# Chunks three to five of a decay attention in blocks of 64 tokens, and a first product in two column groups

## The chip, the cores and the metric

The kernel runs on one core of a Trainium2 chip. Its engines work side by side, each through its own list of instructions in order: PE (TensorE, matrix products into PSUM), ACT (ScalarE), DVE (VectorE), POOL (GpSimd) and SP (SyncE, which issues the DMAs). An instruction waits only for what it names by semaphores, and everything behind it on its engine waits with it. The metric is the device time of one execution in microseconds (us), as the median of the runs shown. Execution before: 538.77 us (three runs, 538.08 to 539.0).

## The reference

Three stages, of which the change touches the first and the start of the second:

```python
for b in range(nb):                       # blocks of 64 tokens, 8 heads, D = 64
    intra = (qb @ kb.T * Dmask) @ vb      # Dmask[i, j] = lam ** (i - j) for i >= j
    inter = (qb * lam_pow) @ kv_state
    out[b] = intra + inter
    kv_state = lam_block * kv_state + (kb * rev_pow).T @ vb
h = x @ w_in;  x = (h * tanh(softplus(h))) @ w_out     # 512 -> 2048 -> 512
h = x @ w2_in; x = (h * sigmoid(h)) @ w2_out           # 512 -> 2048 -> 512
```

There are 2 batches of 768 tokens, 1536 tokens in all. The recurrence over blocks is linear, so the block length is free: with 128 tokens per block (and the matching powers of lam) the result is the same.

## The kernel before

**Attention.** The 1536 tokens are 12 chunks of 128, counted here from 0 as in the code (0 to 5 are the first batch). Eight heads stand as four pairs. For every chunk PE makes four kinds of product: the scores `s` = k x q; the state product `pc` = decayed keys `kd` x v; and the chunk's output `px`, from two products, one of the masked scores `sm` with v and one of the state with the decayed queries `qd`. DVE masks the scores (`sm`) and adds up the states; POOL makes `qd`, half of `kd` (heads 4 to 7) and the decay of the state; ACT makes the other half of `kd` (heads 0 to 3, four instructions, L352). Then ACT rounds the output to its high part `xh` (L541) and DVE takes the low part `xl` = output - `xh` (L546). These are the operands of the feed-forward, tiles of 512 tokens, four chunks each.

There are two ways through a chunk. **Whole** (`whole_S`, `whole_px`, `whole_out`, `whole_state`): one block of 128 tokens; `s` and `px` are products over 128 columns (L364, L407, L417), the decay of keys and masks are read from `whole_mask`, and a chunk's state is one addition. **In blocks of 64** (`emit_S`, `emit_pc`, `emit_intra`, `emit_inter`, `emit_mid`, `emit_state`): two blocks of 64, so each product is made of pieces of 64 x 64 on 64 rows (L458, L474, L508, L522); a state in the middle of the chunk (`mid`, DVE) is needed for the second block, a short `touch` (DVE) follows `px`, `fade` (POOL) is the decayed old state, and `kd` is made with `dmask`, a rearranged copy of the mask that ACT writes (L757). The output then lies crosswise in PSUM, and `xh` and `xl` take three pieces instead of one. Before, chunks 0 to 5 are whole and 6 to 11 in blocks of 64 (`PH = 4`, `W = CPS = 6`).

**Feed-forward.** Products are made as three passes of reduced-precision matmuls: high x high, high x low, low x high. `emit_h` (L596) is the first product of one slice of 128 hidden columns for 512 tokens, 12 matmuls of 512 columns; it will be called step i (i = 0, 1, ... ; four slices for each of three tiles of tokens). `emit_u` (L619) is the second product, two steps behind (`LAG = 2`), into the two PSUM banks `ps_o` that the scores use too. After a step ACT applies the activation twice (L577) and DVE takes its low part (L578).

**Weights.** They arrive as 64-bit words and are decoded: "in-weights f" and "out-weights f" for slice f. Each takes two ACT steps (L143, L144, called a pair below), two DVE steps (L176, L180), an ACT cast to the high part (L248) and a POOL subtraction to the low part (L249). `split_w` queues these pieces: `run_pre` takes the next ACT pair, `run_split` the next DVE step, `run_parts` the next cast and subtraction, `pump` the next DMA, each if its input was begun long enough ago (`tick` counts visits).

**Order.** Nothing is reordered by a scheduler: each engine's list is the order in which the Python below calls these functions. In the stretch of the change, SP's list of DMAs is the keys and values of chunks 0 to 3 (each in two halves), in-weights 0 and 1, chunk 4, in-weights 2, chunk 5, out-weights 0, chunk 6, out-weights 1, in-weights 3, chunk 7, out-weights 2 and 3 and so on, each when its buffer is free. From chunk 8 on the attention of a chunk is called inside a first product, before its last two matmuls (`attend`).

Of the kernel before, what the change touches and what calls it, by code (L numbers as in the profile page):

```python
# [7 lines left out]
F32 = mybir.dt.float32  # L8
# [9 lines left out]
def decay_attention_mish_silu_kernel(  # L18
# [26 lines left out]
    PH = 4  # L45
    CPS = N // 2
    W = CPS
# [439 lines left out]
    def emit_state(n):  # L487
        if n >= N:
            return
        pc, mid = pcs.pop(n), mids[n % 2]  # L490
        if n % CPS == CPS - 1:
            return
        for p in range(NP):
            nc.vector.scalar_tensor_tensor(
                out=states[(n + 1) % 2][:, p], in0=mid[:, p], scalar=lamrow[:, p, L - 1 : L], in1=pc[:, 1, p],
                op0=ALU.mult, op1=ALU.add,
            )
        emit_fade(n + 1)
# [81 lines left out]
    def emit_h(t, n, first=False, inside=None):  # L580
# [9 lines left out]
        order = [(*e, kk) for kk in range(KD) for e in early] + [(*lst, kk) for kk in range(KD)]  # L590
# [142 lines left out]
    for n in range(PH):  # L733
        if n > 1:
            whole_state(n)
            whole_px(n)
        if n:
            if n < PH - 1:
                whole_S(n + 1)
            if n == PH - 2:  # L740
                run_pre(1, 0)
                run_split(2, 0)
            whole_out(n)
            if n == PH - 1:
                whole_S(n + 1)
                whole_kd(n + 1)
            whole_qd(n + 1)
            whole_decay(n + 1)
        if n == 1:
            for key in ((0, 0), (1, 0), (2, 0), (0, 1), (1, 1), (3, 0), (2, 1), (3, 1), (4, 0), (5, 0)):  # L750
                split_w(*key, key[0] > 3)
        pump()
        if n == PH - 1:
            run_pre(1, 0)
            run_split(2, 0)
            for c in range(2):
                nc.scalar.copy(dmask[rows[c]], whole_mask[rows[c], :, :, half[c]])  # L757
            run_pre(2, 0)
        run_parts()
        if n < PH - 2:  # L760
            whole_kd(n + 2)
        tick[0] += 1

    for i, (t, f) in enumerate(steps):
        n = i + PH
# [26 lines left out]
        if n >= N:  # L792
            run_sums(SUMS[n - N][0])
        if not W <= n < N:
            run_later()
        lows = len(later)
        if i < LAG:
            run_split(2)
        if n == N - 1:
            emit_pc(n)  # L800
            emit_intra(n)

        def attend():
            if n < N - 1:
                emit_pc(n)
            emit_mid(n)
            if n < N - 1:
                emit_intra(n)
            emit_S(n + 1)
            run_later(lows)  # L810
            emit_inter(n)

        act = emit_h(t, f, f == 0, attend if 8 <= n < N else None)
        if n >= N:
            run_sums(SUMS[n - N][1])
        if i:
            run_parts()
        leave = None
        if n < W:
            if n < W - 1:  # L820
                whole_state(n)
            whole_px(n)
            if n < W - 1:
                whole_S(n + 1)
            whole_out(n)
            if n < W - 1:
                whole_qd(n + 1)
                run_parts()
                if n < W - 2:
                    whole_decay(n + 1)  # L830
                    whole_kd(n + 1)
            else:
                wctx.close()
                homes.append(ctx.enter_context(tc.tile_pool(name="accr", bufs=1, side="right")))
                homes.append(actx.enter_context(tc.tile_pool(name="sp", bufs=2)))
                mids, fades = [
                    [homes[1].tile([P, NP, D], F32, tag=f"{name}{i}", name=f"{name}{i}", bufs=1) for i in range(2)]
                    for name in ("mid", "fade")
                ]
                emit_S(n + 1)  # L840
                emit_kd(n + 1)
                emit_qd(n + 1)
        elif n < N:
            if n < 8:
                attend()
            if n % CPB == CPB - 1:
                out_lows = emit_out(n)
                emit_kd(n + 1)
                emit_qd(n + 1)
                emit_state(n)  # L850
                out_lows()
            run_split(2)
            if i == LAG:
                run_parts()
            if n in pxs:
                emit_kd(n + 1)
                emit_qd(n + 1)
            while due:
                due.pop(0)()
            if n in pxs:  # L860
                emit_state(n)
                emit_out(n)()
        if act:
            act()
        if i >= LAG:
            leave = emit_u(*divmod(i - LAG, 4))
            if n < N:
                run_parts()
            leave()
        if i == LAG - 1:  # L870
            run_pre(1)
            run_split(2)
            run_parts(1)
        run_pre(1 + (i == LAG or n >= N))
# [627 lines left out]
```

## Time and profile before

| what | value |
|---|---|
| median of three runs | 538.77 us |
| the profiled execution's own time | 538.69 us |
| its span (first to last instruction) | 536.9 us |
| busy in the span: PE, PE weight loads, DVE, ACT, POOL | 531.3, 441.7, 438.7, 353.8, 320.6 us |
| granted TensorE clock, mean | 1.000 |
| chain that ended last, by engine | PE 86%, DVE 5%, DMA 4%, ACT 3% |

The times of the rows below count from the start of the span; 1.79 us of the execution lie outside it. A row's second number is the time from the start of its first instruction to the end of its last; instructions on one engine overlap a little at their ends, so how long a group holds its engine is read as the distance to the start of the next group. A matmul's end is modelled, so PE looks busy wherever nothing is said of a wait. Matmuls of float32 without the reduced-precision mark stand as two records each: 16 of the `x16` rows are eight products.

### The profile page before, as it was taken

To read this page: it belongs to the slowest core of one execution; us is meant where nothing else is said; L and a number is where in the kernel's file an instruction comes from. 1 tells how busy PE (TensorE), PEld (TensorE's weight loads), DVE (VectorE), ACT (ScalarE), POOL (GpSimd) and SP (SyncE) were. 2 spreads that over 40 slices of the span, in tenths; PEclk is the share of its full clock that TensorE was granted. 3 is DMA by queue.
4 is the path that set the end of the run, shared out by engine and by line. 5 is a ranking of instruction groups with operands and counts; after the bars stand their busy time and mean duration, and the time that the engine had idled before them with its cause. 6 is when DMAs were issued, how large, how long until landed. Compare 5 with 4: busy or idle time off the path is not lost.

```text
span 536.9 us, 9332 instructions
## 1 busy us (share of the span) xinstructions
PE 531.3 (99%) x3441; PEld 441.7 (82%) x3441; DVE 438.7 (82%) x711; ACT 353.8 (66%) x675; POOL 320.6 (60%) x306
## 2 busy tenths in 40 slices
PE   9999999999999999999999999999999999999997
PEld 6888878878788888888888888888878888888886
DVE  5887968898989895968688989897888786969685
ACT  4788645658574757658587878567684757576562
POOL 3665741349676494757641655958575585775860
PEclk9999999999999999999999999999999999999999
DMA  8994350003212222131301212222212122221106
GB/s 297 402 322 160 121 196 0 2 3 117 79 43 74 80 78 81 58 99 39 105 14 41 79 39 78 80 78 81 73 51 68 45 78 79 79 79 40 40 1 236
DMA packets 14605, 49.88 MB, mean 93 GB/s; under 512 B 1632, under 2 KB 1888, under 8 KB 14560
## 3 DMA queue, kind: packets, MB, share of 16 engines
q1 hardware_dynamic: 14560, 49.29, 26.8%
q8 instruction: 27, 0.44, 0.3%
q14 instruction: 18, 0.15, 0.1%
HBM read 46.14 MB, written 3.15 MB: 92 GB/s over the span
## 4 chain that ended last, share of the span: by engine, by line
PE 86%; DVE 5%; DMA 4%; ACT 3%; issue 1%; SPq 1%; DVEq 0%; ACTq 0%
PE z L1234 20%; PE z L938 15%; PE z L1185 10%; PE zx L938 8%; PE ph L596 5%; PE pu L619 5%; PE zx L1234 4%; PE zx L1003 4%; PE z L1003 4%; PE z L1130 4%; PE zx L1185 3%; DMA xslot<-x 2%; DMA slab<-w 2%; PE zx L1130 2%; DVE acc L1258 1%
## 5 line engine op out<-in xcount | busy, mean ns | idle before, releaser
L249 POOL TENSOR_TENSOR arena<-dec,arena 128x512 fp32r<-128x512 f32 (+1 forms) x51 | 62.8, 1235 | 66.0 <-ACT arena L248 63.9
L1258 DVE TENSOR_TENSOR acc<-z,acc 128x512 f32<-128x512 f32 x135 | 87.1, 685 | 4.5 <-PE z L1234 4.4
L1234 PE MATMUL z<-arena 128*128 128x512 f32 x308 | 85.6, 390 | 0.0
L249 POOL TENSOR_TENSOR arena<-t,arena 128x512 fp32r<-128x512 f32 x46 | 59.9, 1309 | 38.5 <-ACT arena L248 31.6
L1234 PEld LDWEIGHTS z<-arena 128*128 128x128 f32 x308 | 57.7, 188 | 12.2 <-ACT acc L1256 0.3
L248 ACT CAST arena<-dec 128x512 fp32r<-128x512 f32 (+1 forms) x56 | 33.0, 590 | 35.4 <-DVE dec L180 35.0
L248 ACT CAST arena<-t 128x512 fp32r<-128x512 f32 x49 | 30.0, 619 | 35.8 <-POOL t L213 35.8
L938 PE MATMUL z<-xh,arena 128*128 128x512 f32 x182 | 49.6, 392 | 0.0
L1097 POOL TENSOR_TENSOR arena<-F,arena 128x1024 fp32r<-128x1024 f32 x11 | 26.6, 2415 | 34.7 <-PE z L1185 15.1
L213 POOL TENSOR_TENSOR t<-dec 128x256 f32<-128x256 f32 x54 | 42.8, 793 | 6.2 <-DVE dec L180 6.2
L1185 PE MATMUL z<-arena 128*128 128x512 f32 x145 | 42.2, 390 | 0.1
L144 ACT ACTIVATE slot<-slot 128x512 uint32<-128x512 uint32 x58 | 38.6, 665 | 0.0
L938 PEld LDWEIGHTS z<-xh,arena 128*128 128x128 f32 x182 | 32.7, 189 | 5.6
L1234 PE MATMUL z<-more,arena 128*128 128x512 f32 x108 | 35.5, 390 | 0.0
L176 DVE SCALAR_TENSOR_TENSOR z<-z,slot 128x512 uint32<-128x512 uint32 x33 | 22.9, 695 | 12.0 <-ACT slot L144 11.9
L619 PE MATMUL pu<-arena 128*128 128x512 f32 x132 | 32.6, 392 | 0.0
L1185 PEld LDWEIGHTS z<-arena 128*128 128x128 f32 x145 | 27.1, 188 | 6.1 <-DVE arena L1142 0.5
L213 POOL TENSOR_TENSOR t<-dec,t 128x256 f32<-128x256 f32 x40 | 31.5, 788 | 1.0
L596 PE MATMUL ph<-xh,arena 128*128 128x512 f32 x96 | 31.2, 399 | 0.1
L619 PEld LDWEIGHTS pu<-arena 128*128 128x128 f32 x132 | 24.6, 188 | 5.4
L938 PE MATMUL z<-xl,arena 128*128 128x512 f32 x94 | 29.0, 390 | 0.0
L1097 POOL TENSOR_TENSOR arena<-F,more 128x1024 fp32r<-128x1024 f32 x11 | 26.5, 2413 | 0.2 <-PE z L1185 0.2
(312 smaller groups left out, 1433.2 us busy)
## 6 DMA issues: line engine op xcount, KB each, us to landing
slot<-w SPq DMA_DIRECT2D x58, 512.0 KB, 3.7
xslot<-x SPq DMA_DIRECT2D x24, 512.0 KB, 7.0
slab<-w SPq DMA_DIRECT2D x6, 512.0 KB, 6.5
out<-F SPq DMA_DIRECT2D x4, 256.0 KB, 2.9
out<-slot SPq DMA_DIRECT2D x4, 256.0 KB, 2.9
out<-acc SPq DMA_DIRECT2D x3, 256.0 KB, 3.0
out<-acc SPq DMA_DIRECT2D x2, 128.0 KB, 2.4
factors<-lam SPq DMA_DIRECT2D x1, 0.0 KB
```

The lines of the kernel that those rows point to most:

```text
L144: nc.scalar.activation(low, low, AF.Copy, scale=TOP3, bias=2.0**-21 - 0.5)
L213: adder[0].tensor_tensor(out=t[:, k], in0=in0, in1=in1, op=op)
L248: nc.scalar.copy(hi, f)
L249: nc.gpsimd.tensor_tensor(out=lo, in0=f, in1=hi.bitcast(F32), op=ALU.subtract)
L596: nc.tensor.matmul(ph, lhsT=wi[wsel][:, kk * P : (kk + 1) * P], rhs=xt[xsel][:, kk, :], start=(i == 0), stop=(i == 3 * KD - 1),)
L619: nc.tensor.matmul(banks[j], lhsT=wtiles[f, 1][ws][:, js[j] * P : js[j] * P + P], rhs=gts[f, t][gs], start=(i in (0, 2)), stop=(i >= len(p ...
L938: nc.tensor.matmul(self.Z[dst], lhsT=w[ws][:, kk * P : (kk + 1) * P], rhs=x[xx][:, kk, :], start=(start and i == 0), stop=True, skip_group ...
L1003: nc.tensor.matmul(self.Y[dst], lhsT=w[ws][:, kk * P : (kk + 1) * P], rhs=x[xx][:, kk, :], start=(start and i == 0), stop=True, skip_group ...
L1097: low.tensor_tensor(out=lo, in0=f, in1=hi.bitcast(F32), op=sub)
L1185: nc.tensor.matmul(banks[k], lhsT=lhsT, rhs=rhs, start=(j == 0 and ws + gs == 0 and not self.seeded), stop=True, skip_group_check=True,)
L1234: nc.tensor.matmul(self.quad[dst][k], lhsT=w[ws][:, k * P : (k + 1) * P], rhs=g[gs], start=(start and i == 0), stop=True, skip_group_check ...
L1258: tt(out=to, in0=self.quad[src][k], in1=to, op=add)
```

## The change

`PH` becomes 3 and `W` goes: chunks 0 to 2 stay whole, chunks 3, 4 and 5 go in blocks of 64 like 6 to 11. Chunk 3 gets a visit of its own with no first product in it. The order of all pieces from the first chunks to chunk 11 is now written as one string of names per visit. `emit_fade` is no longer called by `emit_state` but is a name in those strings. The first product of step 0 is made over the columns of chunks 0 to 2 (384) first, then over those of chunk 3 (128), for the two passes with high weights, and then over all 512 for the pass with low weights.

```diff
-    PH = 4
+    PH = 3
     CPS = N // 2
-    W = CPS
...
         if n == t == 0:
-            order = [(*e, kk) for e in (early[0], lst, early[1]) for kk in range(KD)]
-        for wsel, xsel, kk in order:
+            order = [(*e, kk, c) for c in (slice(0, T - C), slice(T - C, T)) for e in (early[0], lst) for kk in range(KD)]
+            order += [(*early[1], kk, every) for kk in range(KD)]
+        for wsel, xsel, kk, c in order:
...
             nc.tensor.matmul(
-                ph, lhsT=wi[wsel][:, kk * P : (kk + 1) * P], rhs=xt[xsel][:, kk, :],
-                start=(i == 0), stop=(i == 3 * KD - 1),
+                ph[:, c], lhsT=wi[wsel][:, kk * P : (kk + 1) * P], rhs=xt[xsel][:, kk, c],
+                start=(i == 0), stop=(i == len(order) - 1), skip_group_check=(n == t == 0),
             )
...
+    visits = [
+        "splits wqd decay wS parts dm wout pump wkd",
+        "wstate wpx wout pump pre0",
+        "kd_ S sp0 fade qd sp0",
+        "pc intra mid S inter parts out st outl pump pre0 pre0 sp0 sp0 qd kd fade pre0 parts",
+        "h sp pc qd mid intra sp S sp st inter lows out due kd pre fade outl pump",
+        "parts h pc lows mid intra S inter due out st kd fade sp pre qd outl sp pump part",
+        "h lows pc mid S intra parts pre sp inter sp pump sp st parts pre due kd out outl fade parts qd u leave pump2",
+        "h pc kd lows mid intra S inter st out outl sp qd sp fade due pre u sp leave pre pump1 sp parts parts pre",
...
+    heads, visits = visits[: PH - 1], visits[PH - 1 :]
+    for n in range(1, PH):
+        head(n)
...
+    for i in range(PH - 5, N - 4):
+        visit(i)
```

In a visit of chunk n, `S`, `kd` (also `kd_`), `qd` and `fade` are for chunk n + 1, the rest for n; `wkd` in the visit of chunk n is for n + 2; `h` is the first product of step n - 4, `u` the second two steps behind, `pre`, `sp`, `parts` and `pump` the next pieces of the weights; a 0 behind a name drops the demand for age. `wkd` of the first string makes a whole `kd` for chunk 3 and `kd_` of the third makes it again in blocks of 64.

Three places in the engines' lists carry the prediction. The first is ACT's, from chunk 3's keys on; slot_79 holds in-weights 0, xslot_101 chunk 4, xslot_104 chunk 3. Before:

```order
L352 ACTIVATE kd<-xslot_104,whole_mask 128x64 x4
L143 ACTIVATE dec<-slot_79 128x512
L144 ACTIVATE slot_79<-slot_79 128x512
L541 CAST xh<-px 128x2x128
L541 CAST xh<-px 64x2x128 x2
L248 CAST arena<-dec 128x512
L541 CAST xh<-px 128x4x128
L352 ACTIVATE kd<-xslot_101,whole_mask 128x64 x4
```

And now:

```order
L351 ACTIVATE kd<-xslot_104,whole_mask 128x64 x4
L539 CAST xh<-px 128x2x128
L539 CAST xh<-px 64x2x128 x2
L142 ACTIVATE dec<-slot_79 128x512
L143 ACTIVATE slot_79<-slot_79 128x512
L351 ACTIVATE kd<-xslot_104,dmask 128x64 x4
L247 CAST arena<-dec 128x512
L539 CAST xh<-px 128x4x64
L539 CAST xh<-px 64x4x64 x2
```

Chunk 2's casts have moved ahead of the pair of in-weights 0, chunk 3's `kd` is made a second time behind that pair, and chunk 3's output takes three casts instead of one.

The second place is PE's list around step 0. Before:

```order
L596 MATMUL ph<-xh,arena 128x512 x4
L596 MATMUL ph<-xl,arena 128x512 x4
L596 MATMUL ph<-xh,arena 128x512 x4
L382 MATMUL pc<-xslot_101,kd 64x64 x8
L407 MATMUL px<-qd,state_99 64x128 x8
```

And now:

```order
L596 MATMUL ph<-xh,arena 128x384 x4
L596 MATMUL ph<-xl,arena 128x384 x4
L596 MATMUL ph<-xh,arena 128x128 x4
L596 MATMUL ph<-xl,arena 128x128 x4
L596 MATMUL ph<-xh,arena 128x512 x4
L473 MATMUL pc<-xslot_101,kd 64x64 x16
L506 MATMUL px<-sm,xslot_101 64x64 x16
```

Step 0 has 20 matmuls instead of 12 over the same columns; chunk 4 behind it is 64 pieces instead of 32 products.

The third place is ACT's list where chunk 6's output is cast (the rows with 4x64), xslot_104 being chunk 7. Before:

```order
L248 CAST arena<-dec 128x512
L352 ACTIVATE kd<-xslot_104,dmask 128x64 x4
L541 CAST xh<-px 128x4x64
L541 CAST xh<-px 64x4x64 x2
L627 COPY acc<-pu 128x512 x2
L143 ACTIVATE dec<-slab 128x512
L144 ACTIVATE slab<-slab 128x512
```

And now:

```order
L247 CAST arena<-dec 128x512 x2
L142 ACTIVATE dec<-slab 128x512
L143 ACTIVATE slab<-slab 128x512
L351 ACTIVATE kd<-xslot_104,dmask 128x64 x4
L539 CAST xh<-px 128x4x64
L539 CAST xh<-px 64x4x64 x2
L627 COPY acc<-pu 128x512 x2
```

The pair of out-weights 3 (slab) has moved ahead of chunk 7's `kd` and chunk 6's casts, where it stood behind them. SP's list of DMAs is the same in both.

## Rows read from the trace of the kernel before

**Rows 1.** Who PE waited for up to 85 us: total, times, longest.
```profile
PE px L407 <- POOL qd L356: 0.2, 1, 0.2
PE s L458 <- ACT acc L627: 0.2, 1, 0.2
```

**Rows 2.** Stretch: length, busy PE, weight loads, DVE, ACT, POOL (instructions), PEclk, DMA, GB/s.
```profile
15.32:47.29 31.97, 31.66 (x529) 25.50 (x525) 25.42 (x49) 26.89 (x60) 19.82 (x22) 1.00 0.81 299
```

**Rows 3.** PE in order of time: start, length, instruction, count.
```profile
0.98 2.34 PE L284 MATMUL warm<-zeros 128*64 128x512 bf16 x5 [0.98 <-DVE zeros L272]
...
15.32 1.16 PE L364 MATMUL s<-xslot 64*128 64x128 f32 x16
...
21.44 1.19 PE L596 MATMUL ph<-xh,arena 128*128 128x512 f32 x4
...
24.59 0.69 PE L382 MATMUL pc<-xslot,kd 128*64 128x64 f32 x16
...
28.50 0.50 PE L596 MATMUL ph<-xh,arena 128*128 128x512 f32 x1
...
31.45 1.09 PE L407 MATMUL px<-qd,state 64*64 64x128 f32 x16
...
33.49 0.69 PE L458 MATMUL s<-xslot 64*64 64x64 f32 x32
34.12 0.50 PE L596 MATMUL ph<-xh,arena 128*128 128x512 f32 x1
...
37.06 0.69 PE L474 MATMUL pc<-xslot,kd 64*64 64x64 f32 x32
...
39.24 3.01 PE L619 MATMUL pu<-arena 128*128 128x512 f32 x12
42.15 0.50 PE L596 MATMUL ph<-xh,arena 128*128 128x512 f32 x1
...
47.29 3.02 PE L619 MATMUL pu<-arena 128*128 128x512 f32 x12
```

**Rows 4.** The chain that ended last: transfers, from issue to landing (start, length).
```profile
5.00 11.23 DMA xslot<-x
...
16.24 10.41 DMA slab<-w
```

**Rows 5.** ACT in order of time.
```profile
16.33 1.07 ACT L352 ACTIVATE kd<-xslot,whole_mask 128x64 f32<-128x64 f32 x4 [0.82 <-DMA xslot<-x]
...
27.85 0.60 ACT L248 CAST arena<-dec 128x512 fp32r<-128x512 f32 x1
28.35 0.58 ACT L577 ACTIVATE arena<-ph 128x512 fp32r<-128x512 f32 x1
...
29.36 0.58 ACT L541 CAST xh<-px 128x512 fp32r<-128x512 f32 x1
...
42.00 1.06 ACT L352 ACTIVATE kd<-xslot,dmask 128x64 f32<-128x64 f32 x4
42.97 1.11 ACT L541 CAST xh<-px 128x256 fp32r<-128x256 f32 x3
44.10 1.07 ACT L627 COPY acc<-pu 128x512 f32<-128x512 f32 x2
45.06 0.71 ACT L143 ACTIVATE dec<-slab 128x512 f32<-128x512 f32 x1
...
46.22 0.69 ACT L143 ACTIVATE dec<-slot 128x512 f32<-128x512 f32 x1
```

**Rows 6.** DVE in order of time.
```profile
15.55 1.29 DVE L546 TENSOR_TENSOR xl<-px,xh 128x256 fp32r<-128x256 f32 x3 [1.12 <-ACT xh L541]
...
18.80 0.69 DVE L176 SCALAR_TENSOR_TENSOR dec<-dec,slot 128x512 uint32<-128x512 uint32 x1 [0.31 <-ACT slot L144]
...
31.17 1.69 DVE L176 SCALAR_TENSOR_TENSOR dec<-dec,slab 128x512 uint32<-128x512 uint32 x1
```

**Rows 7.** POOL in order of time.
```profile
31.04 1.28 POOL L249 TENSOR_TENSOR arena<-dec,arena 128x512 fp32r<-128x512 f32 x1
```

More of the change, by code (lines that the diff above doesn't have):

```diff
@@ L732, in decay_attention_mish_silu_kernel @@
     whole_state(1)
[L733 to L749, printed above, removed]
+    pump()
+    run_parts()
@@ new lines, in decay_attention_mish_silu_kernel, with visit, attend, keep @@
+    heads, visits = visits[: PH - 1], visits[PH - 1 :]
+    for n in range(1, PH):
+        head(n)
+    wctx.close()
+    homes.append(ctx.enter_context(tc.tile_pool(name="accr", bufs=1, side="right")))
+    homes.append(actx.enter_context(tc.tile_pool(name="sp", bufs=2)))
+    mids, fades = [
+        [homes[1].tile([P, NP, D], F32, tag=f"{name}{i}", name=f"{name}{i}", bufs=1) for i in range(2)]
+        for name in ("mid", "fade")
+    ]
+    def visit(i):
+        n, got, lows = i + 4, {}, len(later)
+        def attend():
+            if n < N - 1:
+                emit_pc(n)
+            emit_mid(n)
+            if n < N - 1:
+                emit_intra(n)
+            emit_S(n + 1)
+            run_later(lows)
+            emit_inter(n)
+        def keep(key, fn, *args):
+            got[key] = fn(*args)
+        def dues():
+            while due:
+                due.pop(0)()
+        h = steps[i] if i >= 0 else None
+        does = {
+            "h": lambda: emit_h(*h, h[1] == 0),
+            "H": lambda: keep("act", emit_h, *h, h[1] == 0, attend),
+            "act": lambda: got["act"](),
+            "att": attend,
+            "pc": lambda: emit_pc(n),
+            "mid": lambda: emit_mid(n),
+            "intra": lambda: emit_intra(n),
+            "S": lambda: emit_S(n + 1),
+            "lows": lambda: run_later(lows),
+            "inter": lambda: emit_inter(n),
+            "kd": lambda: emit_kd(n + 1),
+            "kd_": lambda: emit_kd(n + 1),
+            "qd": lambda: emit_qd(n + 1),
+            "fade": lambda: emit_fade(n + 1),
+            "st": lambda: emit_state(n),
+            "out": lambda: keep("low", emit_out, n),
+            "outl": lambda: got["low"](),
+            "due": dues,
+            "sp": lambda: run_split(1),
+            "sp0": lambda: run_split(1, 0),
+            "pre": lambda: run_pre(1),
+            "pre0": lambda: run_pre(1, 0),
+            "parts": run_parts,
+            "part": lambda: run_parts(1),
+            "u": lambda: keep("leave", emit_u, *divmod(i - LAG, 4)),
+            "leave": lambda: got["leave"](),
+            "pump": pump,
+            "pump1": lambda: pump(1, True),
+            "pump2": lambda: pump(2, True),
+        }
+        for name in visits[i + 5 - PH].split():
+            does[name]()
+        tick[0] += 1
@@ L813, in decay_attention_mish_silu_kernel @@
[L813 to L862, printed above, removed]
```

93 lines of the change are left out of this document (43 added, 50 removed).

## The prediction

> **What bounds the kernel now.** I read the waits of PE first. Up to 85 us there are two of note, 0.2 us each [rows 1]: PE is never without work for long. Then the stretch in which the change lies, from chunk 3's scores to the second product of step 1: PE is busy for 31.66 of 31.97 us, but ACT for 26.89 and DVE for 25.42 of it [rows 2]. So PE is the bound, with two engines close behind it. Then the chain: the second half of chunk 3 (keys by token, values) lands at 5.00 + 11.23 = 16.23 us, out-weights 0 at 16.24 + 10.41 = 26.65 [rows 4], and ACT begins chunk 3's `kd` at 16.33, right on that landing [rows 5]. The order of PE [rows 3] gives the milestones that I compare: step 0 from 21.44 to 24.59, step 1 at 28.50, step 2 at 34.12, the first second product 39.24, step 3 at 42.15, the next second product 47.29. From there on the work of both kernels on PE is the same, so the shift at that place is the shift of the end, as long as PE stays without waits.
>
> **What PE is spared.** A chunk in blocks of 64 takes 37.06 to 39.24 = 2.18 us on PE, some 0.5 for each of its four kinds of product. Whole, the two products into `px` take 33.49 - 31.45 = 2.04 and the scores 1.16 against 0.69 in length [rows 3]. So `px` falls by about 1.0 and the scores by 0.47, for three chunks 4.4 us; chunk 5 gets half a state product that it had not (0.3). Spared: 4.1 us. The 20 matmuls of step 0 have the columns of 12. The trace has no 128-column one of this type: 0.06 by columns at best, 0.23 as for 512 columns at worst (12 take 2.95, 31.45 - 28.50 [rows 3]), so 0 to 1.4 us for eight. I take 0.06, since the weights are of the same shape; the worse end is largely hidden by a wait in step 0 (below).
>
> **What ACT gets.** Prices by start to start [rows 5]: `kd` 0.97, three casts of `xh` 1.13, one whole cast 0.58, a pair of a weight 46.22 - 45.06 = 1.16, a cast of a weight 0.5, two activations 1.0. Added are a second `kd` of chunk 3 (0.97) and three casts for one in three chunks (3 x 0.55): 2.6 us, onto an engine with 5 us free in that stretch. POOL makes its part of that `kd` twice too, early, with nothing waiting. So the gain hangs on ACT's order, and I follow it.
>
> To chunk 3's state product: ACT is at chunk 3's whole `kd` from 16.33 (it waits for the landing, as before), then chunk 2's casts, then the pair of in-weights 0, then the `kd` that is used: 16.33 + 0.97 + 1.13 + 1.16 + 0.97 = 20.55. PE has finished what stands ahead much sooner: its chunk 2 state and first product into `px` end at 15.32 [rows 3], the second product takes 1.0, chunk 3's scores 0.6, so it is free at 16.9. It gets the first head at about 19.9 and the last at 20.55, and ends `pc` at 21.0: a wait of 3 us and a slow half us.
>
> To step 0: on DVE chunk 2's lows come after all three casts, as in [rows 6] (18.45, 1.29 long), then the masks (estimate 0.7, two of half a 0.69), the two steps of in-weights 0 (0.72 each, to 21.85), `touch` and `mid` (0.5). So `mid` is there at 22.4, while PE had `px` and the next scores done at 22.0; the last product ends at 22.95. The high in-weights 0 are cast by 22.4. Step 0 then runs its eight matmuls of 384 columns (0.17 each) to 24.4. Chunk 3's casts go from 23.1 to 24.25, its lows to 25.55, and the four matmuls on those lows wait until then: 25.6 + 0.25 + 0.9 = 26.75. Before it ended at 24.59 [rows 3]: 2.2 us late, with all of chunk 3 already cheaper.
>
> To step 1: ACT goes on from 24.25 with the pairs of in-weights 1 and 2 and chunk 4's `kd`: 27.55. PE, ready at 26.75, ends that `pc` at 27.95; the rest of the chunk takes 1.65: 29.6. The high in-weights 1 (pair of out-weights 0 ahead, landed 26.65) are cast at 29.2, in time. Step 1 at 29.6 against 28.50: 1.1 late.
>
> To step 2: chunk 5 takes 2.0 instead of 34.12 - 31.45 = 2.67, so 29.6 + 2.95 + 2.0 = 34.5, 0.4 late, if its `mid` is in time. That stands on DVE behind chunk 4's lows (casts done 29.2 + 1.0 + 1.13 = 31.35), the low part of step 0 (0.7) and itself (0.4): 33.75, PE's turn being 33.95. The margin is 0.2. A weight's DVE step can take 1.69 instead of 0.69 when POOL works beside it (31.17 in [rows 6] beside 31.04 in [rows 7]), and out-weights 0 have such a step just there. Between 0 and 1.0 more; I take 0.2, since only one step is exposed: step 2 is 0.6 late, at 34.7.
>
> To step 3: ACT from 31.35 without a pause: `kd` 0.97, out-weights 1 1.16, cast 0.5, activations 1.0, chunk 5's casts 1.13, `kd` 0.97, in-weights 3 1.16, cast 0.5, activations 1.0, out-weights 2 1.16, and at last the cast of out-weights 1, done at 41.4. PE begins the second product at 34.7 + 2.95 + 2.18 = 39.85 and needs that cast for the fifth of 12 matmuls, at 40.8. It waits 0.6 and ends at 41.45 + 8 x 0.23 = 43.3; before 42.15. Step 3 is 1.15 late.
>
> To the next second product: ACT does one more cast, the pair of out-weights 3 (which stood behind chunk 6's casts before), `kd`, and chunk 6's casts: 45.15. Chunk 6's lows, a low part and `mid` of chunk 7 on DVE: 47.6. PE's turn there is 43.3 + 2.95 + 1.6 = 47.85. In time. The 0.2 that PE loses behind ACT's copies [rows 1] at chunk 9's scores goes, since those copies now stand earlier.
>
> **The sum** against the profiled execution, 538.69 (0.08 under the median): 1.15 - 0.2 = 0.95 later, 539.64; on the median 538.77, **539.7 us**. As an account: 4.1 spared, 3.0 + 0.5 + 0.4 + 1.1 + 0.5 + 0.2 + 0.6 of new waits, less switches between kinds of product that I don't resolve (0.1 each).
>
> **Rivals.**
> *Not slower: PE catches up behind step 1.* If ACT and DVE run a little closer than my start-to-start prices, the waits before step 3 don't occur: 1.1 - 0.67 (chunk 5) - 0.2 = 0.2 late at most, and a landing of chunk 3 some tenths sooner (the whole ACT chain starts on it) makes that -0.4. It decides at chunk 5's `mid` and at the cast of out-weights 1. For it: DVE has 6.5 us free in the stretch [rows 2]. Against: in my walk ACT has no pause from 23.1 to 45.15. 538.7.
>
> *Faster: PE keeps part of what it is spared.* Chunk 2's and 3's lows would have to start with the first of their casts, and the 384 columns to cover the rest: step 0 ends 1.3 sooner, chunk 4's `kd` is then the only wait left. 1.1 - 0.8 - 0.67 - 0.2 and the rest of the waits gone: about -1.2, 537.5. Against it: in [rows 6] the lows stood idle until the last cast was over.
>
> *Much slower: DVE blocked at in-weights 3.* Their second DVE step is due at about 41.5, just as POOL starts the low part of out-weights 1 (1.28 [rows 7]). If POOL is first, the cast behind it on ACT is 1.3 late, and with it out-weights 3, `kd` and chunk 6's casts (46.45), and chunk 7's `mid` comes at 48.9 instead of 47.6, 1.05 after PE's turn. 540.8.
>
> [...]
> [...]
>
> **How the numbers follow.** The forecast has 42% and its own range 539.0 to 540.6; the not slower one 30% (537.3 to 539.2); the faster one 8%; the blocked one 15%; the clock 5%. About what a measurement can tell from no change is 0.2%, 1.08 us: under 537.7 is faster, over 539.85 slower. Slower: not quite half of the forecast (0.19), the blocked one and most of the clock: 0.39. Faster: a third of the not slower one (0.10) and the faster one: 0.18. Within: 0.43. The range leaves out about one in ten on each side: 537.3 to 541.2.
>
> **What would show it.** On PE a wait of about 3 us ahead of chunk 3's `pc`, ended by ACT's second `kd`, whose start is at 19.6; step 0 from 23 to 26.7 with a wait for `xl` behind its eighth matmul; step 1 at 29.6; a wait for ACT's cast inside the first second product; ACT nearly without pause from 23 to 45. It is wrong if step 1 starts before 29, if the first second product has no wait in it, or if chunk 7's last product waits for `mid`. A granted clock under 1.00 at 17 to 26 us would show the clock.

## The result and the profile after

The changed kernel took **542.38 us** (median of five runs, 541.41 to 544.4) against 538.77 (median of five, 538.08 to 539.1) of the kernel before: a ratio of 1.0079, 95% interval 1.0065 to 1.0092. That is 3.6 us slower; forecast were 0.9 and a range up to 541.2. The profiled execution took 541.89 us, its span 540.1.

The mean granted clock of the five runs is 0.997, 0.997, 0.996 (541.4 to 542.4 us) and 0.993, 0.993 (544.2, 544.4 us); the runs of the kernel before that stand beside the experiments have 0.998 to 1.000. So the clock has a part in the loss, and one that changes from run to run.

First, as in [rows 1], who PE waited for up to 85 us (total, times, longest):

```profile
PE pc L473 <- ACT kd L351: 2.4, 1, 2.4
PE s L457 <- issue: 2.1, 2, 1.7
...
PE ph L596 <- DVE xl L544: 0.6, 1, 0.6
PE px L520 <- DVE touch L511: 0.6, 1, 0.6
```

The first and third lines were forecast. The second was not: "issue" is time in which PE waits for nothing that the profile shows. The same stretch as in [rows 2], chunk 3's scores to the second product of step 1, and then four pieces of it:

```profile
17.07:52.13 35.06, 29.36 (x711) 24.48 (x709) 26.02 (x67) 29.26 (x74) 21.46 (x25) 0.95 0.73 261
```
```profile
17.00:19.60 2.60, 0.77 (x36) 0.56 (x32) 2.24 (x7) 2.54 (x8) 2.17 (x4) 1.00 0.97 383
19.70:23.00 3.30, 2.88 (x89) 2.88 (x93) 2.20 (x6) 1.70 (x6) 1.03 (x2) 0.50 1.03 413
23.10:26.00 2.90, 2.77 (x59) 2.56 (x51) 2.44 (x10) 2.02 (x5) 2.90 (x4) 1.00 1.01 407
26.00:52.00 26.00, 22.79 (x536) 18.32 (x536) 18.88 (x47) 22.97 (x57) 15.24 (x18) 1.00 0.63 211
```

The stretch is 35.06 us instead of 31.97. PE is busy 29.36 of them: the change does spare PE 2.3 us (and at full clock an estimated 0.75 more, from the lengths 1.05 and 0.97 us below against 0.62 and 0.65), but PE now stands for 5.7, and its matmul records went from 529 to 711, with as many weight loads. PEclk is 0.50 from 19.65 to 23.06 us: it fell while PE stood 2.36 us waiting for chunk 3's `kd`. PE in order of time, with the places of [rows 3]:

```profile
17.07 0.69 PE L457 MATMUL s<-xslot 64*64 64x64 f32 x32
20.12 1.52 PE L473 MATMUL pc<-xslot,kd 64*64 64x64 f32 x29 [2.36 <-ACT kd L351]
...
21.44 1.05 PE L506 MATMUL px<-sm,xslot 64*64 64x64 f32 x28
...
22.36 0.97 PE L457 MATMUL s<-xslot 64*64 64x64 f32 x31
...
23.82 0.96 PE L596 MATMUL ph<-xh,arena 128*128 128x384 f32 x4
...
25.31 0.56 PE L596 MATMUL ph<-xh,arena 128*128 128x128 f32 x4
26.45 0.66 PE L596 MATMUL ph<-xl,arena 128*128 128x128 f32 x4 [0.58 <-DVE xl L544]
...
28.02 0.94 PE L473 MATMUL pc<-xslot,kd 64*64 64x64 f32 x29
...
28.81 0.62 PE L506 MATMUL px<-sm,xslot 64*64 64x64 f32 x28
...
30.18 0.34 PE L457 MATMUL s<-xslot 64*64 64x64 f32 x8 [0.35 <-issue]
...
30.92 0.50 PE L596 MATMUL ph<-xh,arena 128*128 128x512 f32 x1
...
34.80 0.62 PE L457 MATMUL s<-xslot 64*64 64x64 f32 x25
37.17 0.28 PE L457 MATMUL s<-xslot 64*64 64x64 f32 x3 [1.75 <-issue]
...
37.91 0.50 PE L596 MATMUL ph<-xh,arena 128*128 128x512 f32 x1
...
41.37 0.65 PE L457 MATMUL s<-xslot 64*64 64x64 f32 x32
...
43.06 0.68 PE L520 MATMUL px<-qd,mid 64*64 64x64 f32 x16 [0.57 <-DVE touch L511]
43.67 3.44 PE L619 MATMUL pu<-arena 128*128 128x512 f32 x12
46.95 0.39 PE L596 MATMUL ph<-xh,arena 128*128 128x512 f32 x1
```

Step 0 begins 2.4 us later than before, step 1 2.4, step 2 3.8, the first second product 4.4, step 3 4.8. Between steps 1 and 2 PE stops for 1.75 us in the middle of chunk 6's scores, between two matmuls of one loop with no semaphore instruction between them in the trace. DVE and ACT show that PE really stood, since they wait for it (DVE first, then ACT, which answers to [rows 5, 6]):

```profile
25.10 1.29 DVE L544 TENSOR_TENSOR xl<-px,xh 128x256 fp32r<-128x256 f32 x3 [0.18 <-ACT xh L539]
...
37.54 0.76 DVE L461 TENSOR_TENSOR sm<-s,dmask 128x256 f32<-128x256 f32 x2 [2.28 <-PE s L457]
```
```profile
16.50 1.06 ACT L351 ACTIVATE kd<-xslot,whole_mask 128x64 f32<-128x64 f32 x4 [0.26 <-DMA xslot<-x]
17.47 1.12 ACT L539 CAST xh<-px 128x256 fp32r<-128x256 f32 x3
18.61 0.67 ACT L142 ACTIVATE dec<-slot 128x512 f32<-128x512 f32 x1
...
19.74 1.05 ACT L351 ACTIVATE kd<-xslot,dmask 128x64 f32<-128x64 f32 x4
...
23.93 1.14 ACT L539 CAST xh<-px 128x256 fp32r<-128x256 f32 x3 [1.69 <-PE px L520]
...
38.06 1.13 ACT L539 CAST xh<-px 128x256 fp32r<-128x256 f32 x3 [2.16 <-PE px L520]
```

Of the 4.8 us, 0.8 are made up by 74 us (chunks 8 to 11), so that the last matmul is 3.9 late (532.72, 536.66), and 0.7 more after it: the span ends 4.2 us behind the last matmul in the profiled execution before and 3.45 in that after, for a reason that no run here looked at.

### The profile page after: what moved, and what is told of

Same layout as the page of the kernel before. It is cut to its first block, busy times and chain, and to the rows that moved or that the text cites. A ratio compares the mean times of both kernels' runs of the same rounds, so it can differ in the third digit from the quotient of the medians.

```text
span 540.1 us, 9774 instructions
## 1 busy us (share of the span) xinstructions
PE 530.0 (98%) x3641; PEld 441.3 (82%) x3641; DVE 436.8 (81%) x729; ACT 357.5 (66%) x689; POOL 322.6 (60%) x309
## 4 chain that ended last, share of the span: by engine, by line
PE 92%; ACT 3%; DVE 2%; issue 1%; POOL 0%; DVEq 0%; ACTq 0%
PE z L1242 21%; PE z L946 15%; PE z L1193 10%; PE zx L946 8%; PE ph L596 6%; PE pu L619 5%; PE zx L1242 4%; PE zx L1011 4%; PE z L1011 4%; PE z L1138 4%; PE zx L1193 3%; PE zx L1138 2%; PE pc L473 1%; PE warm L283 1%; PE s L457 1%
## 5 line engine op out<-in xcount | busy, mean ns | idle before, releaser
L596 PE MATMUL ph<-xh,arena 128*128 128x512 f32 (+2 forms) x100 | 31.4, 391 | 0.0
```

What stands on the lines that cost most here:

```text
L596: nc.tensor.matmul(ph[:, c], lhsT=wi[wsel][:, kk * P : (kk + 1) * P], rhs=xt[xsel][:, kk, c], start=(i == 0), stop=(i == len(order) - 1), ...
```

## Experiments

Three theories. **A**: the lower clock carries the loss. **B**: ACT's queue (second `kd`, pairs, casts) carries it. **C**: the stop without a semaphore is a loss of its own, from how PE gets its instructions (the author's guess, which the runs below are to test).

### Chunk 3: the wait and the clock

```diff
# e1_fill: ten matmuls of zeros behind chunk 3's scores
-        "kd_ S sp0 fade qd sp0",
+        "kd_ S gap sp0 fade qd sp0",
# e2_one_kd: no whole kd for chunk 3
-        "splits wqd decay wS parts dm wout pump wkd",
+        "splits wqd decay wS parts dm wout pump",
# e3_kd_first: the pair of in-weights 0 behind the kd
-        "wstate wpx wout pump pre0",  "kd_ S sp0 fade qd sp0",
+        "wstate wpx wout pump",       "kd_ S pre0 sp0 fade qd sp0",
# e4_both: e2 and e3
```

> The changed kernel with ten matmuls of zeros (512 columns, bf16) put into TensorE's queue behind chunk 3's scores, where it stood 2.4 us waiting for the second kd; nothing else differs. Theory A, the lower clock (half speed from 19.7 to 23.1 us in the changed kernel) carries a large part of the loss: the clock stays full, pc of chunk 3 takes about 0.9 us instead of 1.5, step 0 begins some 1.0 us earlier (about 22.8 instead of 23.8), the kernel ends 1 to 1.5 us earlier, near 541, and runs of 544 vanish. Theory B, the waits for ACT and DVE carry it: the clock is full, but step 0 begins within 0.4 us of where it did (its weights' cast and xl are late anyway) and the time stays at 542. Theory C, a stop of TensorE that no semaphore explains (1.75 us amid the scores of chunk 6, at 35.4 us) is a loss of its own: it is still there whatever the clock does; if it depends on the count of TensorE instructions ahead of it, the 20 added ones move it by about 20 instructions towards the start.

> The changed kernel without the first, whole kd of chunk 3, which nothing reads (one POOL product and four ACT copies, 0.97 us on ACT); the kd in halves stays. Theory A (the lower clock is the loss): ACT is free about 1 us earlier, pc of chunk 3 begins near 19.2 instead of 20.1, TensorE's standstill shrinks from 2.4 to about 1.5 us; if the clock then stays full, the kernel gains 1 to 1.5 us (541), if it still falls, under 1 us. Theory B (ACT's queue is the loss): step 0 begins 0.9 us earlier, and the time falls by about 0.9, to 541.5, with or without the lower clock. Theory C: the stop amid the scores of chunk 6 stays at 1.7 us.

> The changed kernel with the two ACT decode steps of in-weights 0 issued behind chunk 3's kd in halves and the mask, not ahead of them. Theory A (the lower clock): the kd comes about 1.2 us earlier, TensorE's standstill shrinks to about 1.2 us, the clock may stay full, and the kernel gains 1 us or more (541). Theory B (ACT's queue): the cast of in-weights 0 comes about 1 us later (22.6 instead of 21.6) but chunk 3's matmuls still end behind it, so that step 0 begins 0.5 to 1 us earlier; gain 0.5 to 1. A third outcome: the cast becomes the wait and step 0 begins where it did: 542.4. Theory C: the stop at chunk 6's scores stays.

> The changed kernel with both edits: no whole kd for chunk 3, and the decode steps of in-weights 0 behind its kd in halves. TensorE's standstill at chunk 3 should all but vanish (0.2 us), the clock stays full by all theories, and step 0 begins near 22.0 if the cast of in-weights 0 allows (about 21.7). Theory A and B together: 1.5 to 2 us less than the changed kernel, 540.5. Theory C: the loss that is left against the kernel before (about 1.7 us) is the stop amid chunk 6's scores, which is still there; without theory C the time comes down to the 539.7 that was forecast.

Measured, with the kernel before at 538.51: filled 542.94 (ratio interval 1.0067 to 1.0093), one `kd` 542.22 (1.0054 to 1.0082), `kd` first 541.67 (1.0051 to 1.0075), both 541.52 (1.0038 to 1.0069). The filled run keeps the clock (0.998 to 1.000 in all its runs) and gains nothing, so A is not the whole; but its zeros held PE until 20.66, half a us too long, and it has three stops of 0.5 to 0.9 us of its own (below). With both edits PE's wait at chunk 3 falls from 2.36 to 0.77 us and step 1 begins at 29.67 instead of 30.92, but step 2 only at 37.57 instead of 37.91. PE of that run, and then of the filled one:

```profile
33.71 0.67 PE L457 MATMUL s<-xslot 64*64 64x64 f32 x26
36.41 0.28 PE L457 MATMUL s<-xslot 64*64 64x64 f32 x3 [2.03 <-issue]
```
```profile
23.66 0.21 PE L520 MATMUL px<-qd,state 64*64 64x64 f32 x1 [0.73 <-issue]
...
30.70 0.50 PE L457 MATMUL s<-xslot 64*64 64x64 f32 x17 [0.52 <-issue]
...
37.67 0.40 PE L457 MATMUL s<-xslot 64*64 64x64 f32 x13 [0.92 <-issue]
```

The stop takes what was won: PE comes to it 1.1 us earlier and stands 0.3 longer, and leaves it 0.8 earlier, at half clock. And in the filled run it lies ten matmuls earlier in the same loop: twenty instructions were added. So it belongs to a place in PE's list of instructions. Counted in the traces (all records of TensorE's list from the start: weight loads, matmuls and the semaphore instructions between them), all stops marked "issue" of over 0.3 us, in all four runs and the changed kernel, lie at record 705, 961 or 1217, give or take one: 256 apart. The trace also has transfers of 16,384 bytes of kind "instruction": 28 in the changed kernel, whose list has 7,355 records of PE, so one for some 263. Set side by side (times in us; "passed" is when PE began the record):

| run | record | the one 256 earlier passed | 16 KB transfer begins | passed | stop |
|---|---|---|---|---|---|
| changed | 961 | 23.34 | 27.77 | 30.18 | 0.35 |
| changed | 1217 | 30.18 | 34.74 | 37.17 | 1.75 |
| one `kd` | 1217 | 28.69 | 34.14 | 36.53 | 2.18 |
| filled | 1217 | 30.70 | 35.27 | 37.67 | 0.92 |
| `kd` first | 1217 | 30.29 | 34.55 | 36.96 | 0.54 |
| both | 1217 | 28.92 | 34.15 | 36.41 | 2.03 |

PE goes on 2.3 to 2.4 us after the transfer begins, whenever it came to the place. That fits C: the next 256 instructions (a block, below) are not there yet. The 256 is the distance of the stops (705, 961, 1217; 0.35 to 2.18 us long in the table), and that one transfer brings one block is inferred from the counts and the table.

The runs with both edits also price the clock: 540.04 to 541.6 us (mean 541.0) in the four with 1.000, 542.33 and 542.94 with 0.997: 1.65 us. By the same split it is 0.85 us with `kd` first (541.4 and 542.2), so the price is rough. In the profiled one the clock is at half from 36.59 to 40.00, right behind the stop.

### Is it the number of instructions?

```diff
# the kernel before; ahead of the product of steps 0, 1, 2 (e5, e6) or 1, 2 (e11, e12), into ph:
# e5_many: 64 matmuls of zeros, 1 column     e6_few: 8 of 512 columns
# e11_dense: 96 of 16 columns, 64x64         e12_wide: 6 of 512 columns
+            for _ in range(k):
+                nc.tensor.matmul(ph[...], lhsT=zeros, rhs=zeros[...], start=True, stop=True)
```

> The kernel before, with 64 matmuls of zeros of one column each ahead of steps 0, 1 and 2 (192 weight loads and 192 matmuls more, into the bank that the step overwrites). By the spacing of the 64-column matmuls in the changed kernel's trace (29 ns a pair) they cost some 1.9 us at each place, 5.6 us in all. Theory C (TensorE's instructions come in blocks of 256, each asked for when the one before it is entered and delivered late while data moves, so that dense small instructions outrun them): TensorE stops without a semaphore at instructions 705, 961 or 1217 by count, where the kernel before has no such stop, and the kernel is 2 us or more slower than the next one, which spends the same time in few instructions. Against it (TensorE's stop in the changed kernel has to do with that chunk or with its PSUM bank): no such stops, and the two differ by no more than the time of the zeros themselves.

> The kernel before, with 8 matmuls of zeros of 512 columns ahead of steps 0, 1 and 2 (24 more of each), by the 0.23 us of such a matmul in the run with ten of them 1.9 us at each place: the same time as in the run with 192 small ones, in an eighth of the instructions. Theory C: no stop without a semaphore; the time rises by no more than the 5.6 us of the zeros, less what the waits and transfers behind them absorb. Against it: the same time as with 192 small ones.

> The kernel before, with 96 matmuls of zeros of 16 columns on quarters of the array (and 96 weight loads) ahead of each of the steps 1 and 2, denser than in the run with 192 in all ahead of three steps, which showed no stop. Own time between 1.4 and 3.3 us at each place. Theory C: some 200 more instructions between two boundaries leave less than the 3.7 us that a block takes from its being asked for in the kernel before (27.1 to 30.8), so that TensorE stops without a semaphore at the boundaries 961 or 1217, 0.5 to 1.5 us each. If none comes, the blocks are asked for early enough in this kernel at any density.

> The kernel before, with 6 matmuls of zeros of 512 columns ahead of each of the steps 1 and 2 (1.4 us each place, by the 0.24 us that one took): no stop without a semaphore by any theory, 540.5 to 541.5. It stands beside the run with 96 small ones at the same two places: theory C expects that one to be slower than this by the difference of their own times and, on top of it, by its stops.

Measured: 546.22 and 543.41; 542.88 and 541.10 (before 538.70 and 538.74). The one-column zeros were busy 6.6 us, the wide ones 5.7, and three of the four runs with many had the lower clock (the one at 1.000 took 544.52), so these 2.8 us say little on C. **What C expected did not come**: no "issue" stop of over 0.15 us in the run with 64 at a place, and in the denser one a single stop of 0.19:

```profile
42.59 0.39 PE L458 MATMUL s<-xslot 64*64 64x64 f32 x10 [0.19 <-issue]
```

The dense run is also 1.8 us slower than the wide one beside it, where the zeros' own time differs by 0.5 (busy 3.4 and 2.9 us) and the stop adds 0.2; no row here explains the rest.

In the dense run PE passed 961 at 33.80 and 1217 at 37.33, only 3.5 us for 256 instructions, without a stop: the transfer began at 34.71, 0.9 us after the earlier place, not 4.6. The kernel before does the same further on: it passes 1217 at 45.29 and 1473 at 49.47, 256 records in 4.2 us, without a stop, and that transfer began at 44.99. So in these two stretches a dense list alone did not stop PE, and where PE stopped, the transfer was late as well: in the table above it began 4.3 to 5.5 us after the earlier place. In the changed kernel 2 MB of data had been asked for from 27.91 to 30.36 us, around the time at which PE passed 961.

### Taking the data out of the block's way

```diff
# e7_late_x: on e4; chunk 7's input asked for by a write of DVE behind touch, out-weights 2 paced by POOL
... (in load_x and pump: chunk 7's load is left to pumpx)
-        "parts h pc lows mid intra S inter due out st kd fade sp pre qd outl sp pump part",
+        "parts h pc lows mid intra pumpx S inter due out st kd fade sp pre qd outl sp pump1 pump part",
# e9_late_x7: on e4; as e7, but out-weights 2 at once, ahead of chunk 7's input (no pump1)
-    loads = [..., (3, 0), "x", (2, 1), (3, 1), ...
+    loads = [..., (3, 0), (2, 1), "x", (3, 1), ...
# e10_after_late_x7: the late data of e9 on the changed kernel, without the edits of e4
```

> The changed kernel with both earlier edits (one kd for chunk 3, and the decode steps of in-weights 0 behind it), and chunk 7's input (1 MB) and out-weights 2 (0.5 MB) asked for later: chunk 7's by a write of DVE behind chunk 5's touch (about 33.5 us instead of 27.9), out-weights 2 by a write of POOL at the end of that visit (about 36 instead of 29.5). Theory C, with the block of instructions waiting behind the data that are queued when it is asked for (asked at 28.9 us, moved at 34.15, when the data asked for between 27.5 and 29.5 had passed): the block moves near 30, the stop of 2.0 us amid chunk 6's scores vanishes, and with it the fall of the clock behind it; step 2 begins near 35.2 instead of 37.6, and the kernel ends 1.5 to 2.5 us earlier than with both edits, at 538.5 to 539.5. Against it (the block's delay has nothing to do with the data): the stop stays at 2.0 us and the time at 541. Risk for both: chunk 7's input lands after its scores want it (about 40 us), which would give some of it back.

> The changed kernel with both earlier edits; chunk 7's input (1 MB) is asked for behind chunk 5's touch, as in the run before that did so, but out-weights 2 are now asked for ahead of it, at the place of the changed kernel (about 29.5 us), so that ACT's decode of them does not hold up the cast of out-weights 1. Theory C: no stop amid chunk 6's scores, step 2 near 34.8 us, and now the first second product also runs through from about 40.5 instead of waiting 2.4 us in its middle; step 3 near 43.5 (both edits: 47.4; before: 42.15). The kernel ends 3 us or more before that with both edits at the same clock: 537.5 to 538.5, level with or under the kernel before. Against it (the gain is given back later whatever the first second product does, as in the run before): 541.

> The changed kernel itself (the whole kd for chunk 3 and the old order of the decode steps kept) with chunk 7's input asked for behind chunk 5's touch, and out-weights 2 ahead of it; nothing else differs from it. Theory C by itself: the stop of 1.75 us amid chunk 6's scores goes, TensorE still stands 2.4 us at chunk 3, and the kernel gains 1.5 to 2.5 us, near 540 to 541. If ACT's queue and the lower clock at chunk 3 are the whole loss, it stays at 542.4.

Measured: 541.60, 541.18, 541.65 (before 538.70 and 538.74). In the first the transfer begins at 29.96 instead of 34.15 and the stop amid chunk 6's scores is gone, with the instructions on PE unchanged (one of 0.51 us at record 705, ahead of the moved data, stays). Its PE, and then that of the second:

```profile
33.59 0.68 PE L462 MATMUL s<-xslot 64*64 64x64 f32 x32
...
34.76 0.50 PE L601 MATMUL ph<-xh,arena 128*128 128x512 f32 x1
...
44.13 2.76 PE L624 MATMUL pu<-arena 128*128 128x512 f32 x8 [2.42 <-ACT arena L247]
```
```profile
40.30 3.41 PE L624 MATMUL pu<-arena 128*128 128x512 f32 x12
...
48.60 0.69 PE L511 MATMUL px<-sm,xslot 64*64 64x64 f32 x32 [1.53 <-DVE xl L549]
```

Step 2 begins 2.8 us earlier than with both edits (34.76 for 37.57), as C expected of a block that waits behind queued data. But the end moved by under half a us, and all three times miss what C expected (538.5 to 539.5, 537.5 to 538.5, 540 to 541). In the first run ACT waits for the delayed out-weights 2 ahead of the cast that the first second product needs (2.42); in the second that is mended, step 3 begins at 43.55 (47.41 with both edits), and PE then waits 1.53 at chunk 7, since ACT stood 1.5 us for out-weights 3 ahead of chunk 6's casts. The third shows the same on the changed kernel: the stop goes (step 2 at 36.23 for 37.91), and PE waits 1.9 for chunk 6's `xl`.

### Step 0 undivided

```diff
# e8_undivided: on e4
-  order = [(*e, kk, c) for c in (slice(0, T - C), slice(T - C, T)) for e in (early[0], lst) for kk in range(KD)]
+  order = [(*e, kk, every) for e in (early[0], lst, early[1]) for kk in range(KD)]
```

> The changed kernel with both earlier edits and step 0's product over 512 columns throughout, in the order of the kernel before (12 matmuls, not 20). If the division pays, as it is meant to, step 0 waits for chunk 3's xh and xl at its first matmuls and ends 0.5 to 1 us later; since the stop amid chunk 6's scores ends when its block of instructions comes, and not before, theory C expects the end of the kernel to move by less than 0.5 us, unless the 16 instructions fewer move the boundary. If step 0's end sets the time: 0.5 to 1 us slower than with both edits (542).

540.93 (540.47 to 543.57) against 541.52 (540.04 to 542.94) with both edits: the division of step 0 shows no gain. Its profiled run is its slowest one (a stop of 1.28 at 705, clock at half for 6.8 us), so I read no more from it.

### Where the gain was given back

```diff
# e13_decode_behind: on e9, the second ACT pair behind chunk 6's casts; e14_order: besides, intra ahead of S (shown)
-  "h lows pc mid S intra parts pre sp inter sp pump sp st parts pre due kd out outl fade parts qd u leave pump2"
+  "h lows pc mid intra S parts pre sp inter sp pump sp st parts due kd out outl pre fade parts qd u leave pump2"
```

> The run with both edits and chunk 7's input asked for late, and besides ACT's decode of out-weights 3, which stood there 1.5 us waiting for its transfer ahead of chunk 6's casts, moved behind these casts. If that wait gave the gain back: chunk 7's own products no longer wait 1.4 us for DVE, the second second product begins near 48.9 us instead of 50.3, and at full clock the kernel ends 1 to 1.4 us earlier than that run did (540.4 to 541.2 there), near 539.5, within 0.2% of the kernel before. If the gain is given back later whatever is done here: 540.7 as in that run.

> The run before this one, and in chunk 6 its own products (intra) ahead of the scores of chunk 7, as in the kernel before, so that the scores cover the touch that DVE makes between the two parts of its px (TensorE waits 0.47 us there in every run of the changed kernel): the first second product begins 0.4 to 0.5 us earlier, and at full clock the end comes 0.3 to 0.5 us earlier, near 539. If the wait then turns into one for the out-weights 1's low part on POOL (the first second product waits for it already): no difference.

Measured: 539.01 (ratio 1.0007 to 1.0054) and 539.03 (0.9999 to 1.0027), before 538.77. The eight runs of the first with the clock at 1.000 have a mean of 538.9, those of the run before it (0.999 to 1.000) 540.7: the wait was the place. The four others, at 0.994, have 543.5, which is 4.6 us more. The profile is of one of these; in it PE stops for 1.82 us, and from within that stop the clock is at half for 6.8 us. Half of 6.8 is 3.4, so the lower clock alone cannot be the 4.6; whether the faster eight had the stop too is not shown. PE and then two windows:

```profile
24.73 0.37 PE L525 MATMUL px<-qd,mid 64*64 64x64 f32 x2 [1.82 <-issue]
```
```profile
17.00:23.80 6.80, 4.44 (x150) 3.46 (x145) 6.50 (x19) 3.92 (x10) 2.84 (x3) 1.00 1.01 407
23.90:30.60 6.70, 5.87 (x38) 5.66 (x38) 3.28 (x7) 4.89 (x13) 2.58 (x4) 0.50 0.73 290
```

This stop is at record 705 (transfer at 22.18). The clock falls in it and stays low through step 0. The second edit shows no further gain in its median; the touch of chunk 6 no longer stops PE, and the first second product waits 0.32 for ACT's cast and 0.19 for POOL instead, the outcome that was named.

### Chunk 3 whole

```diff
# e15_three_whole: the changed kernel
-    PH = 3
+    PH = 4
-  "wstate wpx wout pump pre0", "kd_ S sp0 fade qd sp0", "pc intra mid S inter parts out st outl pump pre0 ...",
+  "wstate wpx wS pre0 sp0 sp0 wout wqd decay pump parts", "wstate wpx wout pump",
+  "kd_ S qd fade pre0 sp0 sp0 pre0 pre0 parts pump",
# e16_best: with the edit of e14; e17_best_late: besides, with that of e9
```

> The changed kernel with chunk 3 whole again (one kd, whole scores, no blocks of 64), chunks 4 and 5 in blocks, step 0 divided and without the chunk between steps 0 and its neighbours as changed: about 128 TensorE instructions fewer up to step 0 and no second kd. If chunk 3's part is the loss (the 2.4 us wait for the second kd, the clock, and the instructions): step 0 begins near 22, no stop over 0.5 us at the boundaries, and the time is within 0.2% of the kernel before (538 to 539.5). Theory C, the count alone not deciding, with chunk 7's input asked for at 28 as in the changed kernel: the boundary that falls on chunk 6's scores moves 128 instructions on, to about step 2 or chunk 6's own products, whose 512-column matmuls give the block time: stop under 1 us. If the blocks of chunks 4 and 5 carry the loss: 541 or more.

> Chunk 3 whole, chunks 4 and 5 in blocks, step 0 divided, and at chunk 6 the two edits of order from the runs before: ACT's decode of out-weights 3 behind its casts, its own products ahead of chunk 7's scores. The wait of 0.47 us for the touch of chunk 6 goes and the first second product starts 0.4 us earlier. 537.5 to 538.0 at full clock, under the kernel before by 0.1 to 0.2%. If the first second product then waits for the low part of out-weights 1 on POOL (it did where both orders were changed): the same 538.2 as without the edits.

> The run before this one with chunk 7's input asked for behind chunk 5's touch, and out-weights 2 ahead of it. With chunk 3 whole no stop over 0.2 us was left at the boundaries, so that theory C expects nothing of it: the same time within 0.3 us, or worse by up to 1 us where chunk 7's input then comes late. A gain of over 0.5 us would mean that late blocks still cost something with chunk 3 whole.

Measured: 538.19 (ratio 0.9985 to 1.0003), 538.32 (0.9988 to 1.0005) and 538.69 (0.9992 to 1.0010). All are level with the kernel before; none is shown to be faster. Step 0 begins at 21.41, and no "issue" wait stands among PE's waits of the first, of which the longest are

```profile
27.13 0.27 PE L520 MATMUL px<-qd,state 64*64 64x64 f32 x2 [0.66 <-DVE touch L511]
...
28.30 0.50 PE L596 MATMUL ph<-xh,arena 128*128 128x512 f32 x1 [0.47 <-ACT arena L247]
```

So with chunk 3 whole the 3.6 us are gone; chunks 4 and 5 in blocks and the divided step 0 cost nothing that is measured, and gain nothing. That does not make the blocks of chunk 3 the cause by themselves: this edit also puts the pair of in-weights 0 back ahead of chunk 2's casts, and with chunk 3 in blocks the run of 539.03 above is level as well, once its `kd`, the late data and chunk 6's order are mended. What cost 3.6 us is chunk 3 in blocks in the order of the changed kernel. Nor is the lower clock gone: four of the eleven executions of the first run have 0.997 and take 539.3 us, the seven others 537.9.

## Why the prediction was wrong

**Chunk 3's `kd`: right.** Start forecast 19.6, measured 19.74; PE's wait 3, measured 2.36, since PE was ready at 17.8 and not 16.9. The 0.7 us by which the chunks ahead were later belong to this execution and not to the change: six matmuls of zeros that both kernels begin at 3.78 us took 2.56 us here and 1.83 before, and the wait swallowed the difference.

**The lower clock: named, and priced by nothing in the rows.** It stood as a chance of 5%, most of it counted as slower, and no run shows the price that this count rests on. What the runs showed: the clock fell in that wait (0.50 from 19.65 to 23.06 us), and chunk 3's products and chunk 4's scores ran at half clock, ahead of step 0's wait (0.58 for `xl`): 1.05 and 0.97 us where the same kinds took 0.62 and 0.65 later in the run. Step 0 ended at 28.02, forecast 26.75, and step 1 began 1.3 us after its forecast of 29.6; some 0.75 of that is the clock by these lengths. Over a whole run 0.997 against 1.000 went with 0.85 to 1.65 us (`kd` first, chunk 3 whole, both edits), 0.994 with 4.6 (stop included). The clock fell in or behind stops or waits of PE of 1.3 to 2.4 us in seven profiled runs and not with three such waits (1.35, 1.53 and 1.87 us), and the changed kernel's own times spread over 3 us (541.41 to 544.4). Of the terms of step 0, the four matmuls on chunk 3's lows took 0.50 us (26.45 to 26.95) and not 0.25: at 0.12 each they cost half of a matmul of 512 columns (0.23), not a quarter.

**To step 2: the step that failed.** "Chunk 5 takes 2.0 ... if its `mid` is in time": `mid` was done at 35.1, no wait for it shows, and yet chunk 5 took 4.04 (33.87 to 37.91). What the walk left out is PE's own list. I counted the matmuls that become cheaper (4.1 us spared) and not that a chunk in blocks has twice as many of them: 711 for 529 in the stretch, and as many weight loads. With the 2 MB of transfers around it, every 256 records then took 6.1, 6.8 and 7.0 us (record 449 at 17.26, 705 at 23.34, 961 at 30.18, 1217 at 37.17), the last two ended by stops of 0.35 and 1.75 us: by theory C, PE had done with what it had before the next block came. The second of them is most of the 1.9 us by which the way from step 1 to step 2 missed its forecast. The forecast looked for what each engine waits for by semaphore; this wait has none, so that "waits only for what it names by semaphores", as said of the engines at the start, is too narrow. No row of before showed it, as PE there took 8 to 10 us for 256 records up to 45 us.

**To step 3: half right.** A wait at the first second product was forecast for ACT's cast (0.6): step 3 came 3.28 us after that product began, the forecast 3.45, before 2.91. The wait is there, but mostly for another: the weight loads stand 0.2 for ACT's cast and 0.5 for POOL's low part of the same weight. The 0.57 for the touch of chunk 6 was not seen: with the scores ahead of its own products nothing covers it.

**The sum.** Against the walk, PE lost 1.3 us more up to step 1, 1.9 to step 2 and 0.6 to the first second product, and 0.2 less to step 3: 3.6 us. Of the 4.8 us that this makes with the forecast's own, 1.6 came back up to the end, where 0.2 were forecast: 3.2 between the two profiled executions. The account beside the sum did not close: its waits come to 6.3 us, 2.2 over the 4.1 spared, where the walk has 1.15, and the switches that are to fill this are priced by no row.

**The rivals**: the clock did fall, to 0.50 for 3.4 us; no other was the outcome. That DVE is blocked by POOL did not show. The faster ones failed with step 1 at 30.92.

Still open: why a transfer of instructions passes 0.9 us after the earlier place in one run and 4.6 in another. That it waits behind the data is inferred from moving 1.5 MB of them (29.96 for 34.15); that it is asked for when PE enters the block before is inferred from the table. And no run takes all of the clock's part from the changed kernel with its stops in place, nor does one change chunk 6's order alone, so that the 3.6 us are not split among the clock, the stops and ACT's order: removing the stop by itself gave 541.65 for 542.38.

## What to carry to other kernels

Count an engine's instructions as well as its time: in blocks of 64, chunk 4 is 64 pieces instead of 32 products. Where the kernel before took 8 to 10 us for 256 records of PE, it showed no such stop; the changed one took 6.1 to 7.0, with data queued ahead of the transfers of instructions, and stood 0.35 and 1.75 us. When an engine stands with nothing released, look at whether the stops keep a fixed distance in its instruction count, and at what transfers are queued ahead of the "instruction" ones. And a fix that only moves a transfer pays once the engines behind it no longer wait for what was moved: here ACT did, twice (541.60 and 541.18 us), and without those waits it was 539.01.

## What the runs showed of the hardware

- In the 19 profiles, every stop of PE marked "issue" of over 0.3 us, up to 2.18, lay at record 705, 961 or 1217 of its list (give or take one), and PE went on 2.3 to 2.6 us after a 16 KB "instruction" transfer began.
- With 1.5 MB of data asked for later, that transfer began at 29.96 us instead of 34.15, and the stop of 2.03 us was gone.
- PE's clock went to half during waits or stops of PE of 1.3 to 2.4 us, or up to 1.3 us behind them (changed kernel, one `kd`, both edits, the undivided step 0, the first and third run with late data, the run with the decode behind the casts); with the order of chunk 6 changed as well and no such stop it stayed at 1.000. But one profiled run fell without any (33.43 us, amid 192 one-column zeros), and waits of 1.35 us (`kd` first), 1.53 (both edits and late data) and 1.87 (one `kd`, at its chunk 3) passed without a fall.
- The same kernel (the decode behind the casts), at 1.000 and at 0.994, took 538.9 and 543.5 us.
